# Gated mix of full and sliding attention: the prologue in five chunks, with other read-outs

## The chip, the cores and the metric

The kernel runs on one core of a Trainium2 chip. A core has five engines that run side by side: TensorE (PE in the profile) multiplies matrices into PSUM, VectorE (DVE) and ScalarE (ACT) compute element by element and read PSUM, GpSimd (POOL) does the same without PSUM, and SyncE (SP) here only issues DMAs. The metric is the device time of one execution in microseconds (us), of which the median of several runs is given. A time below is from the start of the profiled span unless it is called a length.

## The reference

Two attention layers read the same input `x` (1 x 2048 x 640, bf16) and their outputs are mixed by a gate. The core of it:

```python
g = sigmoid((x * gate_w).sum(-1, keepdims=True))
# A: full attention, 32 heads of 20
q, k, v = split(x @ A_wqkv)
a = merge(softmax(q @ k.T * 20**-0.5) @ v) @ A_wo
# B: each position attends to 8 positions, 2 apart, behind it
q, k, v = split(x @ B_wqkv)
idx = pos[:, None] - 2 * arange(8)          # masked where negative
b = merge(softmax(q . k[idx] * 20**-0.5) . v[idx]) @ B_wo
return g * a + (1 - g) * b
```

## The kernel before

The kernel writes every instruction as a task with the buffers that it reads and writes (`T`, L69). A small planner keeps a clock for each engine, and `emit` (L135) writes for each engine its tasks in the order in which they were made, with a semaphore wait for every task of another engine (and for a marked one of its own) on which one depends. So the order of tasks in the source is the order on each engine.

**The main part.** Heads go in eight groups of four ("quads"), queries in four blocks of 512, keys in 16 blocks of 128. One unit is one head, one query block and one key block: a score matmul of 32 rows into a PSUM bank (`mk_qk`, L994), the exponential of that bank on ScalarE (`mk_exp`, L1012), and a value matmul that adds to bank 5 (`mk_pv`, L1018). Units are taken three and two at a time in turn, from banks 0 to 2 and banks 3 and 4, 819 steps in all. Around them a greedy loop (L1175) places "lanes", which are generators with a due time: keys, queries and values of the later quads (`gen_k`, `gen_q`, `gen_v`), late constants and weights (`gen_late`, L594), and the whole of layer B. They share banks 6 and 7.

The softmax needs a bound instead of a row maximum: for every feature of a quad's keys the largest absolute value over all keys (`Kmax`, L409), and from it and the absolute query a bound that is subtracted from the scores. `mk_KM` (L414) takes the largest of the four chunk maxima and multiplies it by -1. `q_km` (L576) multiplies it with `qabs` and adds the result to the query's bank as one more feature, row 0 of each head, whose key is 1 (`e0`). So the first score needs the maximum over all keys of the first quad, and with it all of `x`.

**The prologue**, which the change is about, runs ahead of the planner's loop, in the order that its lines give:

- L320 to L333 issue the loads: from ACT's queue the first quad's key weights (80 columns), its query weights, and the gate vector `gw`; from SP's queue `x` in four chunks of 512 rows (L322), value weights of layer A (`WvA`, L331), the remaining key weights (L332) and query weights (L333). Layer B's weights follow (L595, L596).
- L335 to L360 make constants: the identity for transposes, zeros, ones in the value buffer (`vA`, L359, on VectorE). `pe_warm` (L343) runs ten matmuls on constants in bank 7.
- `pro_tr(t)` (L920) transposes chunk `t` of `x`, 20 blocks of 128 x 128, into three banks (0, 1, 2 or 3, 4, 7 in turn), and reads them out to `xT`: the first bank, two of the five feature blocks, by VectorE (L941), the other two by ScalarE (L938).
- `pro_k(t)` (L944) projects the keys of chunk `t` into bank 6 or 7 with five matmuls (L390), evacuates them to `kT` on ScalarE (L405) and takes their maxima from `kT` on VectorE (L410).
- L950 to L974 give the order: transposes 0 and 1, query weights (L372), keys 0, transposes 2, keys 1, the three Sel constants (`consts_late`, L362, used by layer B), transposes 3, the query matmuls of the first block into bank 0, keys 2, the query's read-out and absolute value (`q_abs`, L569), the gate vector's copy into column 1 of `WvA` (L962), keys 3, KM, six value chunks (`v_chunk`, L468, five matmuls each) in two banks with the KM matmuls between, and their read-outs (`v_evac`, L484, L495 and L503) on ScalarE. Then come the first two score groups (L1168, L1169) and the loop.

Column 1 of `WvA` makes the gate's logit come out of the same matmuls as the values of the first two quads (161 columns instead of 160).

Of the kernel before, what the change touches and what calls it, by code (L numbers as in the profile page):

```python
# [6 lines left out]
BF16 = mybir.dt.bfloat16  # L7
# [225 lines left out]
def _build(ctx, nc, A_x, A_wqkv, A_wo, B_wqkv, B_wo, gate_w, out):  # L233
# [33 lines left out]
    woBp = WvA  # L267
    gw = sb([P, CN], BF16, "gw")
    ident = sb([P, P], BF16, "ident")
# [42 lines left out]
    wB_v = B_wqkv.rearrange("(c p) f -> p c f", p=P)  # L312
    gw_v = gate_w.rearrange("(c p) -> p c", p=P)
    out_v = out[0].rearrange("(b p) d -> p b d", p=P)
# [5 lines left out]
    T("act", lambda e: e.dma_start(WqkA[:, :, D:D + 80], wA_v[:, :, D:D + 80]), writes=[("WkA", 0)], dma=True)  # L320
    for t in range(QCN):
        T("sp", lambda e, t=t: e.dma_start(x_tm[:, 4 * t:4 * t + 4, :], x_v[:, 4 * t:4 * t + 4, :]),  # L322
          writes=[("x_tm", t)], dma=True)
    T("act", lambda e: e.dma_start(WqkA[:, :, 0:80], wA_v[:, :, 0:80]), writes=[("WqA", 0)], dma=True)

    def sp_gw(e):
        with nc.allow_non_contiguous_dma(reason="tiny gate vector"):
            return e.dma_start(gw[:, :], gw_v)

    T("act", sp_gw, writes=["gw"], dma=True)  # L330
    T("sp", lambda e: e.dma_start(WvA[:, :, 2:D + 2], wA_v[:, :, 2 * D:3 * D]), writes=["WvA"], dma=True)  # L331
    T("sp", lambda e: e.dma_start(WqkA[:, :, D + 80:2 * D], wA_v[:, :, D + 80:2 * D]), writes=[("WkA", 1)], dma=True)  # L332
    T("sp", lambda e: e.dma_start(WqkA[:, :, 80:D], wA_v[:, :, 80:D]), writes=[("WqA", 1)], dma=True)  # L333

    T("pool", lambda e: e.iota(itmp, [[1, P]], base=0, channel_multiplier=-1), writes=["itmp"])  # L335
    T("pool", lambda e: e.iota(stmp, [[P, CN], [-DH, 32]], base=0, channel_multiplier=1), writes=["stmp"])
    T("dve", lambda e: e.memset(warm[:, :], 0.0), writes=["warm"])
    T("act", lambda e: e.activation(warm[:, 2:4], warm[:, 0:2], ACTF.Exp), reads=["warm"], writes=["warm2"])
# [4 lines left out]
    def pe_warm(e):  # L343
        ins = None
        for _ in range(10):
            ins = e.matmul(bank[7], ident[:, :], rgn[0][:, :, :].rearrange("p a b -> p (a b)"), start=True, stop=True)
        return ins

    T("pe", pe_warm, reads=["ident", "rgn"], writes=[("bk", 7)])
    T("dve", lambda e: e.memset(zt[:, :], 0.0), writes=["zt"])  # L350
# [3 lines left out]
    for i in range(2):  # L354
# [3 lines left out]
    T("dve", lambda e: e.memset(bank[OB], 0.0), writes=[("bk", OB)])  # L358
    T("dve", lambda e: e.memset(fap(vA, vA[:, 0, 0, 0:1], [[VW, NQUAD * KBN * 4], [1, 1]]), 1.0),  # L359
      writes=[("vA", q, g) for q in range(NQUAD) for g in range(6)])  # L360

    def consts_late():  # L362
        T("dve", lambda e: e.tensor_scalar(stmpf, stmp, 0.0, None, op0=ALU.is_ge), reads=["stmp"], writes=["stmpf"])
        T("dve", lambda e: e.tensor_scalar(Sel[:, :, :], stmp, float(DH), None, op0=ALU.is_ge),
          reads=["stmp"], writes=["Sel"])
        T("dve", lambda e: e.tensor_tensor(Sel[:, :, :], stmpf, Sel[:, :, :], ALU.subtract), reads=["stmpf"], writes=["Sel"])


# [44 lines left out]

    def mk_KM(q):  # L414
        T("dve", lambda e: e.tensor_reduce(Kmax[:, q % 2, 4:5], Kmax[:, q % 2, 0:4], AX.X, ALU.max),
          reads=[("Kmax", q % 2, t) for t in range(4)], writes=[("Kmax", q % 2, 4)], cost=160)
        T("dve", lambda e: e.tensor_scalar(KM[:, q:q + 1], Kmax[:, q % 2, 4:5], -1.0, None, op0=ALU.mult),
          reads=[("Kmax", q % 2, 4)], writes=[("KM", q)], cost=70)

# [48 lines left out]
    def v_chunk(b, p, gi, kb, i_):  # L468
        lo, hi = VG[gi]
        w0, wn = (1, 161) if p == 0 else (2 + 160 * p, 160)  # L470

        def fn(e):
            ins = None
            for c in range(CN):
                ins = e.matmul(bank[b][:, i_ * wn:(i_ + 1) * wn], xT[:, c, kb * P:(kb + 1) * P],  # L475
                               WvA[:, c, w0:w0 + wn], start=(c == 0), stop=(c == CN - 1))
            return ins

        rd = ["xT", "WvA"]
        if i_ == 0:  # L480
            return T("pe", fn, reads=rd, writes=[("bk", b)], cost=375)
        return T("pe", fn, reads=rd, accum=[("bk", b)], cost=375)
# [53 lines left out]
    def gen_k(q):  # L536
        yield ("dve", 370.0, 0.0)
        yield after(mk_wk(q))
        for tcc in range(4):
# [6 lines left out]
            kcount[q] = tcc + 1  # L546
        yield ("dve", 260.0, 0.0)
        mk_KM(q)
# [20 lines left out]
    def q_abs(b, gi):  # L569
        qt = qT[gi % NQT]  # L570
        T("dve", lambda e: e.tensor_copy(qt[:, :], bank[b]), reads=[("bk", b)], writes=[("qT", gi % NQT)], cost=690)  # L571
        return T("dve", lambda e: e.tensor_scalar(qabs[:, :].bitcast(I16), qt[:, :].bitcast(I16), 0x7FFF, None,
                                                  op0=ALU.bitwise_and),
                 reads=[("qT", gi % NQT)], writes=["qabs"], cost=300)
# [19 lines left out]
    def gen_late():  # L594
        T("sp", lambda e: e.dma_start(WqkB[:, :, :], wB_v[:, :, 0:2 * D]), writes=["WqkB"], dma=True)  # L595
        T("sp", lambda e: e.dma_start(WvBraw, wB_v[:, :, 2 * D:3 * D]),  # L596
          writes=["qB", "kB", "WvBraw"] + [("x_tm", t) for t in range(4)], dma=True)
        yield ("s", 4)
        for c in range(CN):
# [4 lines left out]
              cost=1290)  # L604
        latedone[0] = True
        for q in range(NQUAD):
            yield ("dve", 330.0, 0.0)
# [11 lines left out]
        for dp in range(CN):  # L619
            src = bass.AP(tensor=B_wo.tensor, offset=B_wo.offset + dp * D, ap=[[CN * D, 4], [DH * D, 32], [1, D]])  # L620
            T("sp", lambda e, dp=dp, src=src: e.dma_start(woBp[:, dp, 2:D + 2], src), writes=[("woBp", dp), "WvA"], dma=True)
            yield ("s", 2)
# [110 lines left out]
    def gen_F(tc):  # L733

        while not latedone[0] or (tc > 0 and not fdone.get(tc - 1)):
            yield ("poll",)
        xk = [("x_tm", t) for t in range(4)] if tc == 0 else []
        if tc == 0:
# [61 lines left out]
    def gen_K(tc):  # L800
# [3 lines left out]
        if tc == 0:  # L804
            T("dve", lambda e: e.memset(vB4[:, :, 0:PADB], 0.0), writes=["vB4"] + [("x_tm", t) for t in range(4)], cost=100)
        else:
# [113 lines left out]
    def pro_tr(t):  # L920
        bs = (0, 1, 2) if t % 2 == 0 else (3, 4, 7)
        for k, cs in enumerate(((0, 1), (2, 3), (4,))):
            b = bs[k]

            def pe_tr(e, t=t, cs=cs, b=b):
                ins = None
                for ci, c in enumerate(cs):
                    for i in range(4):
                        ins = e.transpose(bank_bf[b][:, ci * 512 + i * P:ci * 512 + (i + 1) * P],  # L929
                                          x_tm[:, 4 * t + i, c * P:(c + 1) * P], ident[:, :])  # L930
                return ins

            T("pe", pe_tr, reads=[("x_tm", t), "ident"], writes=[("bk", b)])
            n = len(cs)
            o_ap = xT[:, cs[0]:cs[0] + n, t * 512:(t + 1) * 512]
            i_ap = bank_bf[b][:, 0:n * 512].rearrange("p (a f) -> p a f", a=n)
            if k != 0:
                T("act", lambda e, o_ap=o_ap, i_ap=i_ap: e.activation(o_ap, i_ap, ACTF.Copy),  # L938
                  reads=[("bk", b)], writes=[("xTt", t, k)])
            else:  # L940
                T("dve", lambda e, o_ap=o_ap, i_ap=i_ap: e.tensor_copy(o_ap, i_ap),  # L941
                  reads=[("bk", b)], writes=[("xTt", t, k)])

    def pro_k(t):  # L944
        b = 6 + t % 2
        mm_part(b, proj_mms(b, WkP[0], t), 0, CN, [("WkP", 0)] + [("xTt", t, k) for k in range(3)], 1100)
        k_evac(b, 0, t, "act")
        k_red(0, t)

    pro_tr(0)  # L950
    pro_tr(1)
    mk_wq(0, 0)
    pro_k(0)
    pro_tr(2)
    pro_k(1)
    consts_late()
    pro_tr(3)
    QB0 = 0
    mm_part(QB0, proj_mms(QB0, WqP[0], 0), 0, CN, [("WqP", 0)] + [("xTt", 0, k) for k in range(3)], 1100)
    pro_k(2)  # L960
    q_abs(QB0, 0)
    T("dve", lambda e: e.tensor_copy(WvA[:, :, 1:2], gw[:, :].rearrange("p (c k) -> p c k", k=1)), reads=["gw", "WvA"],  # L962
      writes=["WvA"], cost=80)
    pro_k(3)
    sch.bufs["xT"] = sch.bufs[("xTt", 3, 2)]
    mk_KM(0)
    for i_ in range(3):
        v_chunk(3, 0, 0, i_, i_)
    q_km(QB0, 0)
    q_cp(QB0, 0)  # L970
    for i_ in range(3):
        v_chunk(4, 0, 1, 3 + i_, i_)
    for gi_ in range(2):
        v_evac(3 + gi_, 0, gi_, "act")  # L974
    for j in range(4):
# [18 lines left out]
    def mk_qk(s, again=0):  # L994
# [12 lines left out]
        for (qc, q, kb, j) in us:  # L1007
            rd.add(("kT", q, kb // 4))
            rd.add(("qT", (qc * NQUAD + q) % NQT))
        T("pe", fn, reads=sorted(rd, key=str), writes=[("bk", b0 + i) for i in range(len(us))], cost=315 + MM * again)  # L1010

# [156 lines left out]
    mk_qk(0)  # L1168
    mk_qk(1)  # L1169
    pend = []  # L1170
    pair_side = 0.0
# [176 lines left out]
```

## Time and profile before

| | us |
|---|---|
| median of three runs | 967.47 (967.17 to 969.41) |
| the profiled execution, its own time | 967.4 |
| its span, first to last instruction | 965.3 |
| busy in the span: TensorE / VectorE / ScalarE | 861.2 / 570.1 / 943.0 |
| first exponential of the main part starts | 22.1 |
| last value matmuls of the main part | 954.8 |
| TensorE idle before value matmuls L475, the first time | 1.4 |

The profile lists groups of equal instructions with busy time, mean length and the idle time of the engine ahead of them. The chain of waits is followed back from the last instruction: at each step to whatever released it. Between 22.1 and 952 us ScalarE is busy 929.0 of 929.9 us. Before 22.1 it is busy 11.1 us, TensorE 18.1 and VectorE 11.8. The DMA engines are busy without a break from about 3 to 24 us, at 280 to 400 GB/s: `x` is 2.6 MB, and the weights queue up behind it.

### The profile page before, as it was taken

The page shows a single profiled execution, that of the slowest core. Times are in us where ns is not written, and L with a number is a line of the kernel's source. Part 1 is how long each engine was busy: PE and PEld are TensorE (multiplying, and loading weights), DVE is VectorE, ACT ScalarE, POOL GpSimd, SP SyncE. Part 2 cuts the span into 40 slices and gives each one's busy share as a digit, 9 for nine tenths or more (in the row PEclk, how much of TensorE's full clock was granted, in tenths as well). Part 3 has the DMA queues.
Part 4 walks back from the last instruction along what each step waited for, and adds up shares of the span by engine and source line. Part 5 has one row for each costly group of instructions (what it writes and reads, how often), then busy time and mean ns, then how long its engine had stood idle before and what let it go on. Part 6 is the DMA issues. An engine that isn't in the chain of part 4 may idle for free.

```text
span 965.3 us, 16312 instructions
## 1 busy us (share of the span) xinstructions
PE 861.2 (89%) x6294; PEld 287.4 (30%) x6397; DVE 570.1 (59%) x1050; ACT 943.0 (98%) x842; POOL 0.7 (0%) x6
## 2 busy tenths in 40 slices
PE   7999999898898888889988889989989998999986
PEld 4333333322222222223322222332222233222332
DVE  4485443445524788762457798355789636987222
ACT  5999999999999999999999999999999999999995
POOL 0000000000000000000000000000000000000000
PEclk9999999999999999999999999999999999999999
DMA  9000000000000000000000000000000000000000
GB/s 312 3 2 21 15 1 1 1 22 14 1 1 1 1 1 1 2 1 7 15 8 1 1 1 1 8 8 7 8 1 1 1 9 14 8 1 1 1 1 28
DMA packets 11359, 12.84 MB, mean 13 GB/s; under 512 B 2708, under 2 KB 10644, under 8 KB 11284
## 3 DMA queue, kind: packets, MB, share of 16 engines
q1 hardware_dynamic: 9028, 11.27, 3.6%
q8 instruction: 52, 0.85, 0.4%
q10 hardware_dynamic: 2256, 0.53, 0.3%
q14 instruction: 23, 0.19, 0.1%
HBM read 9.18 MB, written 2.62 MB: 12 GB/s over the span
## 4 chain that ended last, share of the span: by engine, by line
ACT 73%; issue 17%; PE 8%; DVE 1%; DMA 1%; SPq 0%; DVEq 0%; ACTq 0%
ACT ebuf L1015 72%; PE ps L1002 3%; PE ps L1139 2%; PE ps L390 2%; PE ps L1023 1%; DMA x_tm<-in_A_x_dram 1%; DVE WvB L715 0%; ACT L_sb L838 0%; PE ps L929 0%; PE ps L475 0%; PE ps L765 0%; DVE rg L629 0%; DVE oTn L646 0%; DVE xT L941 0%; ACT kT L405 0%
## 5 line engine op out<-in xcount | busy, mean ns | idle before, releaser
L1015 ACT ACTIVATE ebuf<-ps 128x1536 bf16<-128x1536 f32 (+1 forms) x819 | 929.0, 1374 | 0.8
L1002 PE MATMUL ps<-qT,kT 32*128 32x512 bf16 x2068 | 322.1, 382 | 67.2 <-ACT ebuf L1015 53.6
L1002 PEld LDWEIGHTS ps<-qT,kT 32*128 32x128 bf16 x2068 | 88.9, 91 | 347.3 <-issue 141.6
L1023 PE MATMUL ps<-ebuf,vA 128*21 128x512 bf16 x2048 | 172.0, 382 | 0.6 <-ACT ebuf L1015 0.6
L1139 PE MATMUL ps<-xT,ident 128*128 128x512 bf16 x322 | 125.0, 389 | 16.3 <-PE ps L1002 6.3
L895 DVE TENSOR_TENSOR bw<-vB,bw 128x640 f32<-128x640 bf16 x112 | 91.8, 820 | 2.1
L899 DVE TENSOR_TENSOR blkacc<-blkacc,bw 128x640 f32<-128x640 f32 x96 | 79.0, 823 | 2.9
L629 DVE STREAM_TRANSPOSE rg<-ps 128x512 f32<-128x512 f32 x32 | 22.9, 717 | 93.4 <-PE ps L1023 93.4
L781 DVE TENSOR_TENSOR prod<-qk 128x512 bf16<-128x512 bf16 x160 | 57.3, 418 | 20.0 <-PE ps L765 19.8
L1139 PEld LDWEIGHTS ps<-xT,ident 128*128 128x128 bf16 x366 | 35.1, 96 | 98.9 <-PE ps L1139 59.3
L1023 PEld LDWEIGHTS ps<-ebuf,vA 128*21 128x21 bf16 x2048 | 42.0, 90 | 72.8 <-issue 50.3
L390 PE MATMUL ps<-xT,WqkB 128*128 128x512 bf16 x179 | 58.2, 384 | 2.2 <-PE ps L1002 1.4
L750 DVE CAST qk<-ps 128x512 bf16<-128x512 f32 x40 | 27.5, 687 | 48.1 <-PE ps L390 46.1
L390 PE MATMUL ps<-woA_r,oTn 128*128 128x320 bf16 x240 | 50.6, 302 | 0.1
L390 PE MATMUL ps<-xT,WqP 128*128 128x512 bf16 x148 | 43.1, 382 | 1.6 <-issue 0.6
L571 DVE CAST qT<-ps 128x512 bf16<-128x512 f32 x32 | 22.0, 688 | 37.7 <-PE ps L390 37.7
L390 PE MATMUL ps<-xT,WkP 128*128 128x512 bf16 x147 | 42.6, 382 | 1.9 <-issue 1.3
L402 DVE TENSOR_SCALAR kT<-ps,e 128x512 bf16<-128x512 f32 x28 | 21.0, 749 | 39.4 <-PE ps L390 39.3
L588 DVE CAST qT<-ps 128x512 bf16<-128x512 f32 x32 | 22.0, 688 | 23.2 <-PE ps L581 23.2
L390 PE MATMUL ps<-WvA,oBacc 128*128 128x320 bf16 x160 | 33.1, 301 | 0.5 <-PE ps L1002 0.4
L475 PE MATMUL ps<-WvA,xT 128*128 128x160 bf16 (+1 forms) x320 | 29.3, 233 | 1.4 <-DVE WvA L962 1.4
L813 DVE CAST vB<-ps 128x512 bf16<-128x512 f32 x20 | 13.7, 687 | 26.8 <-PE ps L390 26.5
(92 smaller groups left out, 471.9 us busy)
## 6 DMA issues: line engine op xcount, KB each, us to landing
x_tm<-in_A_x_dram SPq DMA_DIRECT2D x4, 640.0 KB
out_dram<-outsb SPq DMA_DIRECT2D x12, 160.0 KB
WqkB<-in_B_wqkv_dram SPq DMA_DIRECT2D x1, 1600.0 KB
WqkA<-in_A_wqkv_dram SPq DMA_DIRECT2D x2, 700.0 KB
WvA<-in_A_wqkv_dram SPq DMA_DIRECT2D x1, 800.0 KB
qk<-in_B_wqkv_dram SPq DMA_DIRECT2D x1, 800.0 KB
woA_r<-in_A_wo_dram SPq DMA_DIRECT2D x32, 25.0 KB
WvA<-in_B_wo_dram SPq DMA_DIRECT2D x5, 160.0 KB
```

Source lines behind the costliest of these rows:

```text
L390: ins = e.matmul(o, l, r, start=(k0 + k == 0), stop=(k0 + k == n - 1))
L475: ins = e.matmul(bank[b][:, i_ * wn:(i_ + 1) * wn], xT[:, c, kb * P:(kb + 1) * P], WvA[:, c, w0:w0 + wn], start=(c == 0), stop=(c == CN - 1))
L571: T("dve", lambda e: e.tensor_copy(qt[:, :], bank[b]), reads=[("bk", b)], writes=[("qT", gi % NQT)], cost=690)
L629: return T("dve", lambda e: e.transpose(rg[i][:, :], bank[OB]), reads=[("ob", j) for j in range(4)], writes=["rg"], cost=720)
L750: give(b, T("dve", lambda e, dst=dst, b=b: e.tensor_copy(dst, bank[b]), reads=[("bk", b)], writes=[key], cost=690))
L781: t = T("dve", lambda e, r=r, f=f, off=off: e.tensor_tensor(prod[r][:, :], qB[:, f, :], kB[:, f, off:off + 512], ALU.mult), reads=["qB", " ...
L895: T("dve", lambda e, vv=vv, av=av: e.tensor_tensor(tmpB, vv, av, ALU.mult), reads=[("aT", ai), "vB4"], writes=["tmpB"], cost=822)
L899: T("dve", lambda e: e.tensor_tensor(blkacc[:, :, :], blkacc[:, :, :], tmpB, ALU.add), reads=["tmpB"], writes=["blkacc"], cost=822)
L1002: ins = e.matmul(bank[b0 + i], kT[32 * j:32 * j + 32, q, kb * P:(kb + 1) * P], qT[gi % NQT][32 * j:32 * j + 32, :], start=True, stop=True)
L1015: return T("act", lambda e: e.activation(ebuf[s % NEB][:, 0:512 * n], ps[:, b0 * 512:(b0 + n) * 512], ACTF.Exp, scale=SCALE), reads=[("bk" ...
L1023: ins = e.matmul(bank[OB][32 * j:32 * j + DH + 1, :], vA[:, q, kb, VW * j:VW * j + DH + 1], ebuf[s % NEB][:, i * 512:(i + 1) * 512], start ...
L1139: T("pe", lambda e: e.matmul(bank[b], ident[:, :], xT[:, 0, 0:512], start=True, stop=True), reads=["xT", "ident"], writes=[("bk", b)], cos ...
```

## The change

All of it is in the prologue and in a few tasks that move out of it.

- `x` comes in five chunks of 256, 512, 512, 512 and 256 rows, and transposes, keys and maxima follow these chunks. A chunk of 512 uses banks 2, 3, 4 or 0, 1, 4 in turn, read out by VectorE, ScalarE and VectorE; a chunk of 256 uses banks 0 and 1, with three feature blocks read out by VectorE and two by ScalarE.
- Ten warm-up matmuls in bank 7 become seven in bank 0.
- Keys of all chunks but the last two are evacuated and reduced as before (bank 7). Those of the last two (banks 4 and 3) are reduced straight from PSUM; their evacuations by ScalarE follow the reductions.
- The first query block is projected later, behind keys 2, in two halves of 256 into banks 5 and 6, and is read out from both by one instruction. Its KM matmuls go by halves; one half is read out by VectorE and one by ScalarE.
- KM is one reduction without the factor -1; instead `qabs` gets its sign bit set where it was cleared.
- The gate vector is loaded straight into column 1 of `WvA`, without a copy. The load of `WvA` is split: 160 columns for the first two quads ahead, the others behind.
- Of the six value chunks three stay ahead of the first scores (bank 7, the third one behind the KM matmuls), and three go behind the first two score groups (bank 6, read out by VectorE).
- The ones in `vA` are written by POOL; the Sel constants are made in `gen_late`, behind the value weights of layer B.

```diff
-    for t in range(QCN):
-        T("sp", lambda e, t=t: e.dma_start(x_tm[:, 4 * t:4 * t + 4, :], x_v[:, 4 * t:4 * t + 4, :]),
+    CH = ((0, 256), (256, 512), (768, 512), (1280, 512), (1792, 256))
+    NCH = len(CH)
+    for t, (o_, n_) in enumerate(CH):
+        T("sp", lambda e, a=o_ // P, z=(o_ + n_) // P: e.dma_start(x_tm[:, a:z, :], x_v[:, a:z, :]),
           writes=[("x_tm", t)], dma=True)
...
-    T("act", sp_gw, writes=["gw"], dma=True)
-    T("sp", lambda e: e.dma_start(WvA[:, :, 2:D + 2], wA_v[:, :, 2 * D:3 * D]), writes=["WvA"], dma=True)
+    T("act", sp_gw, writes=["WvA1"], dma=True)
+    T("sp", lambda e: e.dma_start(WvA[:, :, 2:162], wA_v[:, :, 2 * D:2 * D + 160]), writes=["WvA0"], dma=True)
+    T("sp", lambda e: e.dma_start(WvA[:, :, 162:D + 2], wA_v[:, :, 2 * D + 160:3 * D]), writes=["WvA"], dma=True)
...
+    T("pool", lambda e: e.memset(fap(vA, vA[:, 0, 0, 0:1], [[VW, NQUAD * KBN * 4], [1, 1]]), 1.0),
+      writes=[("vA", q, g) for q in range(NQUAD) for g in range(6)])
...
-        for _ in range(10):
-            ins = e.matmul(bank[7], ident[:, :], rgn[0][:, :, :].rearrange("p a b -> p (a b)"), start=True, stop=True)
+        for _ in range(7):
+            ins = e.matmul(bank[0], ident[:, :], rgn[0][:, :, :].rearrange("p a b -> p (a b)"), start=True, stop=True)
...
+    def mk_KM(q, n=4):
+        T("dve", lambda e: e.tensor_reduce(KM[:, q:q + 1], Kmax[:, q % 2, 0:n], AX.X, ALU.max),
+          reads=[("Kmax", q % 2, t) for t in range(n)], writes=[("KM", q)], cost=160)
...
+        if n == 512:
+            parts = zip(((0, 1), (2, 3), (4,)), (2, 3, 4) if t % 2 else (0, 1, 4), ("dve", "act", "dve"))
+        else:
+            parts = zip(((0, 1, 2), (3, 4)), (0, 1), ("dve", "act"))
...
+    KB = (7, 7, 7, 4, 3)
...
+    def pro_kev(t):
+        a, n = CH[t]
+        b = KB[t]
+        return T("act", lambda e: e.activation(kT[:, 0, a:a + n], bank[b][:, 0:n], ACTF.Identity, bias=e0[:, 0:1]),
+                 reads=["e0"], accum=[("bk", b)], writes=[("kTt", t)])
...
+    def pro_k(t):
+        a, n = CH[t]
+        pro_kmm(t)
+        pro_kev(t)
+        pro_red(t, kT[:, 0, a:a + n], reads=[("kTt", t)])
+    def pro_k2(t):
+        pro_kmm(t)
+        pro_red(t, bank[KB[t]][:, 0:CH[t][1]], reads=[("bk", KB[t])])
+    QH = (OB, 6)
+    def pro_q():
+        for h in range(2):
+            b = QH[h]
+            mms = [(bank[b][:, 0:256], WqP[0][:, c, :], xT[:, c, 256 * h:256 * h + 256]) for c in range(CN)]
+            mm_part(b, mms, 0, CN, [("WqP", 0)] + xkeys[0] + xkeys[1], 600)
...
     pro_tr(0)
     pro_tr(1)
+    pro_k(0)
     mk_wq(0, 0)
-    pro_k(0)
     pro_tr(2)
     pro_k(1)
-    consts_late()
     pro_tr(3)
...
+    pro_tr(4)
     pro_k(2)
...
+    pro_q()
+    pro_k2(3)
+    pro_k2(4)
+    mk_KM(0, NCH)
+    pro_kev(3)
+    pro_kev(4)
+    for i_ in range(2):
+        v_chunk(7, 0, 0, i_, i_)
+    for h in range(2):
...
+        T("pe", fn, reads=["qabs", ("KM", 0)], accum=[("bk", b)], cost=MM)
...
+    v_chunk(7, 0, 0, 2, 2)
+    v_evac(7, 0, 0, "act")
...
     mk_qk(0)
     mk_qk(1)
+    for i_ in range(3):
+        v_chunk(6, 0, 1, 3 + i_, i_)
+    free_at[6] = v_evac(6, 0, 1).fin + 56.0
```

## The prediction

> **What bounds the kernel now.** I read the page first: its busy shares, the chain that ended last by engine, and the costliest group.
>
> ```profile
> span 965.3 us, 16312 instructions
> PE 861.2 (89%) x6294; PEld 287.4 (30%) x6397; DVE 570.1 (59%) x1050; ACT 943.0 (98%) x842; POOL 0.7 (0%) x6
> ACT 73%; issue 17%; PE 8%; DVE 1%; DMA 1%; SPq 0%; DVEq 0%; ACTq 0%
> L1015 ACT ACTIVATE ebuf<-ps 128x1536 bf16<-128x1536 f32 (+1 forms) x819 | 929.0, 1374 | 0.8
> ```
>
> ScalarE's 819 exponentials cost 929.0 us, and ScalarE stood idle 0.8 us before all of them together. Once they run, nothing can be won but that 0.8. So a change to the prologue is worth what it moves the first exponential, unless it makes the later order stall. The chain of waits, cut to the first 26 us, shows what sets that first one:
>
> ```profile
> 1.24 6.82 DMA x_tm<-in_A_x_dram
> ...
> 14.24 2.12 PE ps L390 x9
> 16.36 0.02 issue
> 16.38 0.70 ACT kT L405
> 17.08 0.02 issue
> 17.10 0.69 DVE Kmax L410
> 17.79 0.61 DVE qT L571
> ...
> 18.63 0.18 DVE WvA L962
> 18.81 0.05 issue
> 18.86 1.23 PE ps L475 x15
> 20.09 0.31 PE ps L581 x4
> 20.40 1.18 PE ps L475 x15
> 21.58 0.02 issue
> 21.60 0.57 ACT vA L495
> 22.18 0.06 ACT zg L503
> 22.24 4.52 ACT ebuf L1015 x4
> ```
>
> Columns: start, length, what. The reader is to see the end: a key evacuation, a maximum, the query read-outs, the gate copy, value matmuls, the max correction, more value matmuls, a value evacuation, then the first exponential at 22.24. Between the maximum's start (17.10) and that lie 5.14 us of short serial steps. The timeline of TensorE shows the front:
>
> ```profile
> 1.42 4.45 PE L346 MATMUL ps<-rgn,ident 128*128 128x512 bf16 x10 [1.42 <-DVE e L351]
> 5.69 1.66 PE L929 MATMUL ps<-ident,x_tm 128*128 128x128 bf16 x20
> 8.10 1.29 PE L929 MATMUL ps<-ident,x_tm 128*128 128x128 bf16 x20 [0.75 <-DMA x_tm<-in_A_x_dram]
> ```
>
> Ten warm-up matmuls start 427 ns apart. The first 20 transposes take 1.66 us, the next 1.29: counting starts in slices of 0.3 us, their pace doubles near 6.3 us, 4.9 us after TensorE began. The granted clock reads 1.00 in these slices all the same, so pace is the witness here.
>
> **The change, part by part.** I re-time the prologue by hand with the rows of before.
>
> *Five chunks of x.* Before, chunks land at 5.69 or just before, 8.05, 10.4 and 12.55 (waits of transposes for x): 0.64 MB each 2.35 us. At that pace rows to 256, 768, 1280, 1792 and 2048 land at about 4.5, 6.85, 9.25, 11.5 and 12.55. The last byte is no earlier; the last piece is half as large. One more x issue (0.45 to 0.88 us on SP) and one more for the split value weights push only the weights behind x on SP's queue: by the bytes moved, the key weights of the second quad are in at about 16 to 18, and their first reader stands at 21.06 before, some 19.5 now.
>
> *Seven warm-up matmuls.* They end 3 x 0.427 = 1.28 us earlier, at about 4.4; the first x then lands at 4.5. Ten cold transposes (0.107 each) run 4.5 to 5.6, then TensorE idles until 6.85. If the pace has doubled by then, transposes of chunk 1 end at 8.15, keys 0 at 8.75, transposes of chunk 2 run 9.25 to 10.55, keys 1 (5 x 0.216 = 1.08) to 11.6, chunk 3 to 12.9, chunk 4 (half of 1.29) to 13.55, keys 2 to 14.63. Keys 2 end at 16.36 before, since the query matmuls stood ahead of them; that is 1.7 us won.
>
> *Read-outs.* VectorE's 1024-wide one costs 0.69, ScalarE's 1.02 and 0.59 for 512. VectorE's 512 and 768 are not in the trace; they lie between the 0.17 of a five-element copy and 0.69, and I take 0.4 and 0.55, near the 0.39 of the 400-element copy and the 0.69 row. VectorE is then free at 14.75, ScalarE at 14.3. Key evacuation 2 runs 14.65 to 15.35, its maximum 15.4 to 16.1.
>
> *Query in two banks.* Ten half-width matmuls cost 1.08 if width decides (10 x 0.108) and 2.16 if each costs as much as a whole one; weight loads take 0.098 each in the row of L390, so I take 1.08: 14.63 to 15.75, hidden behind the maximum. Were it 2.16, query would end at 16.8 and keys 3 and 4 at 18.5, 0.7 late. The read-out from two banks (0.68) runs 16.1 to 16.8, the sign operation (0.29) to 17.1.
>
> *Maxima from PSUM.* Keys 3 end at 16.8 and keys 4 (half) at 17.35, both hidden behind VectorE. Reading 512 from PSUM in a maximum is not in the trace: between 0.68 (cast from PSUM) and 0.75 (L402), I take 0.69, and 0.42 for the last 256 (between 0.16 for four and 0.68 for 512): 17.1 to 17.8 to 18.2. The joined KM operation saves one of two 0.16 steps: KM at 18.36, against 19.76. The new wait: evacuations 3 and 4 on ScalarE now come after the maxima, 17.85 to 18.55 and (0.4) 18.95; behind them in ScalarE's queue stand the second query read-out, the value evacuation and the first exponential.
>
> *Gate column by DMA.* L962's copy (0.17) goes; value matmuls no longer wait for it but for two DMAs, and the KM matmuls stand behind them in TensorE's queue. The gate DMA lands 10.5 us after its issue at 1.88, at 12.4, and nothing needs it before 17.35. The new piece of value weights is 200 KB, behind x: at 375 GB/s it lands at 13.1; as slow as the 100 KB query weights of 160-byte rows (8.5 us) it lands at 21.0. I take 14, near the first bound, since it follows x on the same queue. A landing after 18.4 delays the end one for one, so the far bound costs 2.6 us.
>
> *The end.* Two value chunks (0.82) are done by 18.2, KM matmuls (0.31) run 18.45 to 18.8, the query halves are read out by VectorE to 19.2 and by ScalarE (0.4) 18.95 to 19.35; the third value chunk ends at 19.2. Score matmuls run 19.4 to 19.8. ScalarE's value evacuation (0.57 and 0.06) ends at 19.98, and the first exponential starts at 20.05. Three value chunks and an evacuation that stood on the path now follow the second score group; their 1.23 us fit where TensorE waited before (0.5 and 0.95 us idle ahead of the second and third score groups), with evacuation on VectorE, idle 4.33 us there. Without this cover the third exponential waits up to 0.7.
>
> *Off the path:* the ones of the value buffer go to POOL, busy 0.7 us in all; from 0.3 to 4 us (between a POOL iota of 160 elements at 0.27 and eight times VectorE's 0.485), needed at 19.4. Three Sel constants (0.8 us) go into the main part, where VectorE is 59% busy. One KM step fewer per quad saves nothing, as VectorE doesn't bound.
>
> Sum: 22.24 - 20.05 = 2.2 us. My hand-offs are near zero and rows say 0.02 to 0.25, so I allow 0.3 for a dozen: 1.9. The profiled run is 967.4 (span 965.3 and 2.1 around it), the median 967.47: 967.4 - 1.9 = 965.5.
>
> The pages bear on two places. "TensorE: Matmul & The Clock Gate", section "The HAM clock gate", of the Trainium skill says that half rate ends after a busy window of about 3.4 us whose phase is not tied to the kernel's start. It speaks against fewer warm-up matmuls: a window holding the new idle time might not count, and the estimate would be some 966.4 instead of 965.5. The trace agrees on halving (427 ns against 216), and shows 4.9 us to the rise.
>
> "DMA: Bandwidth & Descriptors", section "Specifications", wants pieces of 512 bytes or more for line rate; the 320-byte rows of the new weight piece break that. No run here shows what they cost.
>
> **The rivals.**
>
> *The clock rises later.* For: between 5.6 and 6.85 TensorE would idle before it has been busy 4.9 us. Against: a pause of 0.75 us before 8.10 left the pace fast. From 6.85 each microsecond at half pace makes TensorE half a microsecond late, less 0.5 that the wait for chunk 2 absorbs. If counting starts afresh at 6.85, the rise is at 11.75: (11.75 - 6.85)/2 - 0.5 = 1.95 lost, 967.4. A rise at 9.7, between the two, loses (9.7 - 6.85)/2 - 0.5 = 0.9: 966.4. Chance 0.27 for 966.0 to 967.4.
>
> *Slower: TensorE stays at half pace through the prologue.* Same place, but past 11.9 us, where loss equals gain, it is slower than before. The price at worst is the 10 us of matmuls from 6.85 to the last keys, taken twice, less 0.5 and less 0.45 that keys 4 wait for VectorE anyway: 9 us lost, 7 net, 974.5. Against: continuous work from 6.85 is longer than the 4.9 us that sufficed before. Chance 0.11 for 967.5 to 974.5.
>
> *More than I see.* If chunks land sooner (x moves at 300 GB/s before, 390 later) and ScalarE's tail is shorter, the first exponential comes at 19.2: 964.4, or with the 0.8 us idle gone 963.6. For: half the last chunk. Against: VectorE's queue from 15.4 on depends little on landing. Chance 0.18 for 963.0 to 964.8.
>
> *The value weights land late* (21.0): 965.5 + 2.6 = 968.1. Chance 0.03.
>
> **How the numbers follow.** The forecast case, 964.8 to 966.0, has 0.41. The range reaches down into the third rival and up past the whole first and the late weights: 964.0 to 968.4. A measurement of this kernel can tell about 0.3%, or 2.9 us, from no change: faster than 964.5 gets 0.16 (most of the third rival), slower than 970.4 gets 0.08 (the worse half of the second), the rest 0.76.
>
> **What would show it.** The first exponential near 20 us in the chain; KM near 18.4; transposes of chunk 1 in 1.3 and not 2.1 us; keys 2 ending near 14.6; the two maxima on PSUM at 0.69 and 0.42, back to back after the sign operation; no wait of value matmuls for a DMA; idle time before the exponentials still about 0.8 us. The main part's order is generated anew; if that idle time grows by more than 1 us, or the pace doubles after 9 us, the prediction is wrong.

## The result, and the profile after

| | before | after |
|---|---|---|
| median of 12 runs each, us | 968.45 (967.17 to 970.05) | 965.64 (964.40 to 967.39) |
| ratio, 95% interval | | 0.9972 (0.9964 to 0.9980) |
| profiled execution, its time / span | 967.4 / 965.3 | 965.52 / 963.7 |
| first exponential of the main part | 22.12 | 19.51 |
| from it to the last quad's L629 | 933.1 | 934.1 |

The change takes 0.28% (0.20 to 0.36), or 2.8 us. The forecast was 965.5, from 967.4. Two executions below stand outside all medians and spans, one of the kernel before (1253.58 us) and one of the variant with one warm-up matmul (1752.59 us). The page of the changed kernel, the lines that answer to those of before:

```profile
span 963.7 us, 16441 instructions
PE 881.2 (91%) x6408; PEld 287.5 (30%) x6408; DVE 570.4 (59%) x1047; ACT 941.6 (98%) x839; POOL 3.1 (0%) x7
L1076 ACT ACTIVATE ebuf<-ps 128x1536 bf16<-128x1536 f32 (+1 forms) x819 | 929.5, 1370 | 1.3
```

The main part's exponentials cost what they did (929.0 before); the idle time ahead of them rose from 0.8 to 1.3. Now the chain of waits, from the third x chunk to the first exponential (start, length, what):

```profile
1.74 7.58 DMA x_tm<-in_A_x_dram
9.33 0.05 issue
9.37 1.29 PE ps L934 x20
10.66 1.08 PE ps L386 x5
11.74 1.68 PE ps L934 x30
13.42 1.09 PE ps L386 x5
14.51 0.02 issue
14.53 0.70 ACT kT L961
15.23 0.02 issue
15.25 0.69 DVE Kmax L965
15.94 0.61 DVE qT L990
16.55 0.02 issue
16.57 0.29 DVE qabs L992
16.86 0.94 DVE Kmax L965 x2
17.81 0.02 issue
17.83 0.17 DVE KM L411
18.00 0.04 issue
18.05 0.38 PE ps L1020 x8
18.43 0.47 PE ps L469 x5
...
18.99 0.57 ACT vA L489
19.56 0.06 ACT zg L497
19.62 6.46 ACT ebuf L1076 x6
```

The reader is to see that keys 2 (L386, 13.42) now end at 14.51 and not at 16.36, that both last maxima (L965 x2) come straight behind the sign operation (L992), that no gate copy is left, and that one value chunk (L469 x5) stands in this chain where two groups of three (L475 x15) stood before.

The profile has one thing more. The main part is 1.0 us longer than before. I compared the starts of L629, the transposition that ends each of the 32 groups: after minus before is -2.47 to -2.49 us for the first nine, -1.31 for the tenth, -1.57 for the eleventh and between -1.44 and -1.79 from there on. The loss is one event, and busy times by stage show it (columns: stretch, its length, busy time and instructions of PE, PEld, DVE, ACT and POOL, granted clock, DMA share, GB/s):

```profile
300.00:306.00 6.00, 5.69 (x41) 1.80 (x38) 3.80 (x3) 6.00 (x6) 0.00 (x0) 1.00 0.01 3
306.00:308.00 2.00, 0.98 (x6) 0.24 (x5) 0.71 (x1) 2.00 (x4) 0.00 (x0) 1.00 0.00 0
308.00:309.00 1.00, 0.68 (x10) 0.37 (x12) 1.00 (x1) 1.00 (x2) 0.00 (x0) 0.93 0.00 0
309.00:312.00 3.00, 3.00 (x21) 0.45 (x14) 0.77 (x2) 2.86 (x3) 0.00 (x0) 0.50 0.00 0
312.00:313.00 1.00, 1.00 (x9) 0.20 (x8) 0.30 (x1) 0.95 (x2) 0.00 (x0) 0.87 0.00 0
```

At 306.00 ScalarE computes layer B's exponential (L838) between two of the main part's; TensorE, which waits for the next one, is busy 0.98 of 2 us. Then its granted clock falls to 0.50: with 0.93 in 308 to 309 and 0.87 in 312 to 313 it is low for 0.14 + 3 + 0.26 = 3.4 us, and ScalarE is no longer busy throughout. The profile of before has the same hole behind its L838 at 308.5, and no fall.

### The profile page after: what moved, and what is told of

It reads as the page before. It is cut to its first block, busy times and chain, and to the rows that moved or that the text cites. A ratio compares the mean times of both kernels' runs of the same rounds, so it can differ in the third digit from the quotient of the medians.

```text
span 963.7 us, 16441 instructions
## 1 busy us (share of the span) xinstructions
PE 881.2 (91%) x6408; PEld 287.5 (30%) x6408; DVE 570.4 (59%) x1047; ACT 941.6 (98%) x839; POOL 3.1 (0%) x7
## 4 chain that ended last, share of the span: by engine, by line
ACT 73%; issue 17%; PE 8%; DVE 1%; DMA 1%; SPq 0%; DVEq 0%; ACTq 0%
ACT ebuf L1076 72%; PE ps L1061 2%; PE ps L1200 2%; PE ps L386 1%; PE ps L1084 1%; DMA x_tm<-in_A_x_dram 1%; DVE WvB L715 0%; ACT L_sb L838 0%; PE ps L934 0%; DVE Kmax L965 0%; DVE rg L629 0%; DVE oTn L646 0%; PE ps L765 0%; DVE rgn L643 0%; PE ps L865 0%
## 5 line engine op out<-in xcount | busy, mean ns | idle before, releaser
L1200 PE MATMUL ps<-xT,ident 128*128 128x512 bf16 x366 | 142.0, 389 | 9.7
L629 DVE STREAM_TRANSPOSE rg<-ps 128x512 f32<-128x512 f32 x32 | 22.9, 717 | 94.8 <-PE ps L1084 94.8
L386 PE MATMUL ps<-xT,WqkB 128*128 128x512 bf16 x200 | 64.1, 387 | 0.0
L386 PE MATMUL ps<-woA_r,oTn 128*128 128x320 bf16 x240 | 50.6, 302 | 0.0
L386 PE MATMUL ps<-xT,WqP 128*128 128x512 bf16 (+1 forms) x165 | 45.6, 376 | 0.7 <-DVE WqP L368 0.5
L386 PE MATMUL ps<-xT,WkP 128*128 128x512 bf16 (+1 forms) x165 | 45.5, 376 | 0.0
L582 DVE CAST qT<-ps 128x512 bf16<-128x512 f32 x31 | 21.4, 689 | 22.2 <-PE ps L575 22.1
L386 PE MATMUL ps<-WvA,oBacc 128*128 128x320 bf16 x160 | 33.1, 301 | 0.4 <-PE ps L1061 0.4
L386 PE MATMUL ps<-xT,WvB 128*128 128x512 bf16 x100 | 31.7, 380 | 0.0
```

The source lines that it names most:

```text
L386: ins = e.matmul(o, l, r, start=(k0 + k == 0), stop=(k0 + k == n - 1))
L582: return T("dve", lambda e: e.tensor_copy(qT[gi % NQT][:, :], bank[b]), reads=[("bk", b)], writes=[("qT", gi % NQT)], cost=690)
L629: return T("dve", lambda e: e.transpose(rg[i][:, :], bank[OB]), reads=[("ob", j) for j in range(4)], writes=["rg"], cost=720)
L1200: T("pe", lambda e: e.matmul(bank[b], ident[:, :], xT[:, 0, 0:512], start=True, stop=True), reads=["xT", "ident"], writes=[("bk", b)], cos ...
```

## The experiments

Times are medians, with the ratio to runs of the kernel before on the same chip. "First" is the start of the first exponential in the profile, "KM" the start of that instruction; 19.51 and 17.83 in the changed kernel, 22.12 and (its first step) 19.41 before. One profile of a variant is one draw, and the next run shows how far two draws differ. Fences of edits are shortened to the lines that matter.

**The changed kernel again.**

> The changed kernel once more, for a second profile. Theory: the prologue's gain repeats (first exponential of the main part at 19.3 to 19.8 us, 22.1 before), and the 1.2 us that the main part lost between 307 and 313 us, where the granted TensorE clock read 0.50, is chance: this time it is absent or at another place, and the main part from the first to the last exponential lasts 932.4 to 933.8 us. Rival: the main part's newly generated order loses it, so the loss of 1.2 us stands at the same place again.

965.56 us, ratio 0.9967 (0.9954 to 0.9980). Half of it missed: the fall at 308 is absent and the main part lasts 933.3 us to the last L629, but the first exponential came at 20.26, KM at 18.58. TensorE's timeline (start, length):

```profile
4.74 1.22 PE L934 MATMUL ps<-ident,x_tm 128*128 128x128 bf16 x10
6.93 2.31 PE L934 MATMUL ps<-ident,x_tm 128*128 128x128 bf16 x20 [0.96 <-DMA x_tm<-in_A_x_dram]
10.10 1.31 PE L934 MATMUL ps<-ident,x_tm 128*128 128x128 bf16 x20
```

and in the first profile of the same kernel:

```profile
4.74 0.86 PE L934 MATMUL ps<-ident,x_tm 128*128 128x128 bf16 x10
7.05 1.29 PE L934 MATMUL ps<-ident,x_tm 128*128 128x128 bf16 x20 [1.45 <-DMA x_tm<-in_A_x_dram]
```

Twenty transposes in 2.31 us are half pace: here the pace doubled only at about 10.2 us, in the other profile at about 5.1. That is the rival "the clock rises later", in one and the same kernel, and it costs 20.26 - 19.51 = 0.75 us. So TensorE's clock comes in twice: in the prologue of the changed kernel, and in holes of the main part.

**Fillers in layer B's holes.**

```diff
-  ... ACTF.Exp, scale=SCALE), reads=["L"], writes=["L"], cost=1060)
+  ... ACTF.Exp, scale=SCALE), reads=["L"], writes=["L"], cost=1060); [idle_mm() for _ in range(4)]
```

> The changed kernel with four added filler matmuls on TensorE at each of the four places where ScalarE computes layer B's softmax exponential (L838) between two of the main part's. Theory: the 0.9 us hole that L838 leaves on TensorE can let its clock fall to half for 3.4 us, which costs about 1.2 us when it happens; filled, the granted clock stays at 1.00 from 20 to 950 us in the profile, the times spread less than the 3 us of the changed kernel, and the median is 0.3 to 1.2 us lower than the changed kernel's. Rival: fillers delay the score matmuls behind them or change nothing in the clock: median equal or up to 1 us higher, spread as before.

965.87 us, 0.9966 (0.9953 to 0.9978). The profile has no fall from 20 to 950 us, and five times spread over 1.35 us, but the median is no lower: inconclusive on the time. Three of its five spans (964.0 to 964.3) still lie about 1 us above the other two (962.9 and 963.2); no trace shows what those three lost. The fillers' own price shows: the main part lasts 933.6 where kernels without a fall have 933.1 to 933.3 (0.36 of it at the sixteenth group, behind the second place).

**A further version.** Edit, on top of the fillers:

```diff
-    pro_k(2)
+    pro_k2(2)
+    pro_kev(2)
     pro_q()
...
-    for i_ in range(2):
-        v_chunk(7, 0, 0, i_, i_)
+    v_chunk(7, 0, 0, 0, 0)
...
-    v_chunk(7, 0, 0, 2, 2)
-    v_evac(7, 0, 0, "act")
...
     mk_qk(1)
+    for i_ in range(1, 3):
+        v_chunk(7, 0, 0, i_, i_)
+    free_at[7] = v_evac(7, 0, 0).fin + 56.0
```

> The filled kernel, with chunk 2's maximum also taken from PSUM (its evacuation behind it), one value chunk instead of three ahead of the first scores, and all value read-outs of the first two groups on VectorE. Theory: VectorE's queue bounds KM, and ScalarE's value read-out delays the first exponential; KM moves from 17.8 to about 17.45 and the first exponential from 19.5 to 19.0, so 0.5 us less than the filled kernel. Rival: TensorE's keys 3 and 4 bound KM, and the first scores end no sooner: 19.4 to 19.6.

965.96 us, 0.9966 (0.9954 to 0.9978): no better. The first exponential came at 19.39, KM at 17.76. The rival is right:

```profile
15.64 1.04 PE ps L386 x4
16.68 0.02 issue
16.70 0.70 DVE Kmax L965
...
18.07 0.47 ACT kT L961
18.54 0.28 ACT qT L1029
18.82 0.14 issue
18.96 0.59 PE ps L1059 x5
```

Maximum 3 starts when keys 3 (L386) end, so TensorE is the next bound, and ScalarE's evacuations behind the maxima hold the second query half. Five value chunks behind the second score group also bring the third exponential's scores into the chain, at a cost of 0.03 us.

**One warm-up matmul instead of seven.**

```diff
-        for _ in range(7):
+        for _ in range(1):
```

> The changed kernel with one warm-up matmul instead of seven. Theory of the clock: TensorE idles from about 1.9 to 4.7 us and again to 7.05, so its pace doubles only at 10 to 12 us; transposes of chunk 1 take 2.1 us instead of 1.3, and the first exponential comes 1.2 to 2 us later, at 20.8 to 21.6. Rival: the pace doubles at a time that does not depend on the warm-up: first exponential at 19.3 to 19.8, as with seven.

966.24 us over seven executions, 0.9975 (0.9965 to 0.9986). As the theory of the clock has it: first exponential at 21.46, two chunks at half pace:

```profile
6.98 2.32 PE L934 MATMUL ps<-ident,x_tm 128*128 128x128 bf16 x20 [1.30 <-DMA x_tm<-in_A_x_dram]
10.15 2.34 PE L934 MATMUL ps<-ident,x_tm 128*128 128x128 bf16 x20
13.53 1.84 PE L934 MATMUL ps<-ident,x_tm 128*128 128x128 bf16 x30
```

1.95 us later than with an early rise, 1.20 later than with the late one.

The eighth execution, of 1752.59 us (span 1750.7), has a mean granted clock that reads 1.000 where the seven others read 0.998, and no trace. TensorE is busy 859.6 us in the profile of this variant, nearly all of it at full pace; twice that, some 1720 us as an estimate, fits a TensorE that stayed at half pace to the end, with the clock reading 1.00 as it does here ahead of the rise. This would be the prediction's second rival, far beyond its worst price of 974.5. Whether the single warm-up matmul brought it about, one execution can't show.

**Parts of the change undone, one at a time.**

```diff
# order_back
-    pro_k(2)
-    pro_q()
+    pro_qmm()    # the query's matmuls
+    pro_k(2)
+    pro_qrd()    # its read-out and sign
# max_back
-    pro_k2(3); pro_k2(4); mk_KM(0, NCH); pro_kev(3); pro_kev(4)
+    pro_k(3); pro_k(4); mk_KM(0, NCH)
# values_back
+    for i_ in range(3):
+        v_chunk(4, 0, 1, 3 + i_, i_)
     v_evac(7, 0, 0, "act")
+    v_evac(4, 0, 1, "act")
...
     mk_qk(1)
-    for i_ in range(3):
-        v_chunk(6, 0, 1, 3 + i_, i_)
-    free_at[6] = v_evac(6, 0, 1).fin + 56.0
# four_chunks
-    CH = ((0, 256), (256, 512), (768, 512), (1280, 512), (1792, 256))
+    CH = ((0, 512), (512, 512), (1024, 512), (1536, 512))
...
-        for _ in range(7):
+        for _ in range(10):
...
```

> The changed kernel with the query's ten matmuls ahead of keys 2 again; VectorE's order stays. Theory: keys 2 then end 1.1 us later, and everything behind their maximum on VectorE with them: maximum 2 at 16.3, KM at 18.9, first exponential at 20.6 (1.1 later than 19.5). Rival: the maxima from PSUM are what pays, and VectorE catches up: first exponential at most 0.4 later.

> The changed kernel with the maxima of the last two key chunks taken from their evacuated copies again, as for the other chunks. Theory: keys 3 end at 16.5, their evacuation at 17.25, the two maxima at 18.4, so KM comes 0.5 later (18.4); ScalarE is free earlier, so the first exponential comes 0.4 to 0.5 later, at 20.0. Rival: with evacuations out of the way of ScalarE's second query half, nothing is lost: 19.4 to 19.6.

> The changed kernel with all six value chunks ahead of the first scores and both read-outs on ScalarE. Theory: the three added chunks (1.23) stand in TensorE's queue ahead of the first scores, and the second read-out ahead of the first exponential: 20.7, 1.2 later. Rival: they fit where TensorE waits for KM, at most 0.3 later.

> The changed kernel with x in four chunks of 512 rows and ten warm-up matmuls, as before; the last chunk's maximum is taken from PSUM. Theory: the last 512 rows land at 12.55 and their 20 transposes end 0.6 to 0.7 later than with a short last chunk, so keys 2, the maxima and the first exponential come 0.5 to 0.6 later, at 20.1. Rival: one reduction less on VectorE makes up for it: 19.5 or sooner.

| run | median, ratio (95%) | KM | first | later than 19.51 | expected |
|---|---|---|---|---|---|
| order_back | 966.87, 0.9981 (0.9970 to 0.9992) | 19.09 | 20.76 | 1.25 | 1.1 |
| max_back | 965.94, 0.9968 (0.9956 to 0.9979) | 18.50 | 20.17 | 0.66 | 0.4 to 0.5 |
| values_back | 967.93, 0.9991 (0.9980 to 1.0002) | 17.84 | 20.52 | 1.01 | 1.2 |
| four_chunks | 965.95, 0.9974 (0.9964 to 0.9984) | 18.20 | 19.87 | 0.36 | 0.5 to 0.6 |

All four profiles have the pace doubled before chunk 1, so the first exponentials compare. Each theory holds within 0.25 us and each rival falls, by the first exponential; the times alone (intervals of some 2 us) could not tell max_back or four_chunks from the changed kernel. (before_early_fill, below, has the prologue of before unchanged and its first exponential at 22.26 instead of 22.12: two draws of one prologue differ by 0.14 even where the clock rises early in both.) The four losses add to 3.28, more than the whole 2.61: the parts overlap. order_back's profile has a fall too, from 309.8 to 313.2 us, behind L838 as in the first profile of the changed kernel; after_again, one_warm, max_back and four_chunks have the same hole and no fall.

values_back lost more time than its 1.0 us. Its main part is 935.5 long, and its clock fell twice, first here (same columns):

```profile
22.50:23.00 0.50, 0.34 (x4) 0.25 (x4) 0.00 (x0) 0.50 (x2) 0.00 (x0) 0.87 1.08 376
23.00:26.00 3.00, 3.00 (x13) 0.86 (x12) 0.89 (x2) 2.64 (x3) 0.00 (x0) 0.50 0.51 173
```

just behind the hole which the value chunks fill in the changed kernel, and again at 650.9, behind L838.

**Parts of the change alone, in the kernel before.**

```diff
# before_order
+    pro_k(2)
     mm_part(QB0, proj_mms(QB0, WqP[0], 0), ...)
-    pro_k(2)
     q_abs(QB0, 0)
# before_max: pro_k2 reduces from the bank, makes KM, then evacuates
-    pro_k(3)
+    pro_k2(3)
...
-    mk_KM(0)
# before_order_max: both
```

> The kernel before with one edit: keys 2 projected ahead of the query. Theory (each part of the change is worth little alone, because another queue is late next): maximum 2 comes 1.0 earlier, but maximum 3 still waits for the evacuation of keys 3 and comes 0.5 earlier, and the value matmuls stand ahead of the scores: first exponential 0.6 to 0.7 earlier, at 21.5 (22.1 before). Rival: the 1.7 us that keys 2 are earlier in the changed kernel come from the order alone, and the end follows: 20.5 to 20.8.

> The kernel before with one edit: the last chunk's maximum taken from PSUM, its evacuation behind it. Theory: nothing is won, as VectorE reaches that maximum at 18.7 only, 0.5 after the evacuation's end: first exponential at 22.0 to 22.2. Rival: a step of 0.7 leaves the chain: 21.4 to 21.6.

> The kernel before with both of these edits. Theory: KM comes 0.9 earlier (18.5), but the value matmuls then stand in front: first exponential 0.8 to 1.0 earlier, at 21.2, more than the two edits' sum by 0.2 to 0.3. Rival: both together bring most of the change's 2.6: 20.0 or sooner.

| run | median, ratio (95%) | first | earlier than 22.12 | expected |
|---|---|---|---|---|
| before_order | 967.72, 0.9990 (0.9979 to 1.0000) | 21.61 | 0.51 | 0.6 to 0.7 |
| before_max | 968.37, 0.9993 (0.9984 to 1.0002) | 22.33 | -0.21 | 0 |
| before_order_max | 968.12, 0.9987 (0.9978 to 0.9997) | 21.14 | 0.98 | 0.8 to 1.0 |

The maximum from PSUM alone wins nothing (its -0.21 is hardly more than the 0.14 between two draws), the order alone 0.5, both 1.0: each step uncovers the queue behind it. before_order_max's profiled run then lost 2.3 us between the first exponential and the first L629 (its clock read 0.50 from 24.1 to 30.9 us), so its 0.98 was gone again in that run.

**Fillers in the early hole of the kernel before.** The hole is TensorE's two waits ahead of the second and the third score group, in the profile of before:

```profile
22.38 0.39 PE L1002 MATMUL ps<-qT,kT 32*128 32x512 bf16 x2 [0.49 <-ACT zg L503]
23.72 0.40 PE L1002 MATMUL ps<-qT,kT 32*128 32x512 bf16 x3 [0.95 <-ACT ebuf L1015]
```

```diff
-    mk_qk(1)
+    mk_qk(1); T("pe", ...)    # four matmuls of ident and xT into bank 7
```

> The kernel before with one edit: four filler matmuls between the second and the third score group, where TensorE idles 0.49 and 0.95 us and where the changed kernel puts three value chunks. Spans of the kernel before fall on three levels, about 965.4, 966.4 and 967.8 us, with mean clocks of 0.998, 0.9965 and 0.9945. Theory: one of the two falls of the clock that a 967.8 span holds starts in this hole (as at 22.9 and 24.2 us in two profiles of kernels with all values ahead of the scores), and the value chunks that moved there also took this fall away. Then no span is above 967.0, and the median of times is 0.5 to 1.3 us lower than that of the kernel before. Rival: the falls come from layer B's exponentials alone; spans near 967.8 remain in a third of the runs, and the median is within 0.4.

967.61 us, 0.9990 (0.9980 to 0.9999), 0.6 below the median of before measured beside it (968.24). Eleven of twelve spans are 965.4 to 965.8, one is 967.1; of 16 spans of before on that chip seven are 965.4 to 965.6, five 966.3 to 966.6 and four 967.6 to 967.9. In these runs filling the early hole thus took away most of the time lost on the upper levels. My statement that none is above 967.0 failed by one run, and that both levels go, not only the upper one, is more than I expected: why a filled early hole also spares the later falls stays open.

## Why the prediction was right

**The number.** That 965.64 lies so near 965.5 is in part luck. In the first profile the prologue won 2.61 and not 1.9, the main part lost 1.0 that the prediction put at nothing, and the time around the span was 1.8 instead of 2.1. In the second the pace doubled after 9 us, which the prediction had named as a sign of being wrong; the time was 965.78 all the same, since that main part had no fall.

**The bound.** Right: a change to the prologue is worth the first exponential's move, 2.61 us in the first profile and 1.86 in the second. Wrong was "nothing can be won but that 0.8" in the main part. Idle time ahead of exponentials in one profile without a fall does not show what a fall takes in another run: 0.9 to 1.1 us, or 2.3 in the long one. Over all experiments, spans of the kernel before lie on three levels near 965.5, 966.5 and 967.8, about a third of 82 runs on each, with mean clocks of 0.998, 0.9966 and 0.9943. One fall of 3.4 us lowers the mean over 966 us by 0.0018 and two by 0.0035 (an estimate), which fits one and two falls; the kernel before itself has a trace of the lowest level alone. The changed kernel's 17 spans are 962.6 to 962.9 (three) and 963.6 to 963.9 (fourteen). From lowest level to lowest level (965.5 to 962.8) that is 2.7 us, from mean to mean (966.6 and 963.6) 3.0. The 967.47 that the prediction stood on, and its profile, came from the lowest level of before; twelve runs gave 968.45. So 1 us of the 2.8 is the kernel before being slower than its three runs said.

**The sum.** It gave 20.05 and allowed 0.3 on top; the first profile has 19.62 in the chain's terms. Chunks landed 0.04 to 0.2 later than worked out (7.05, 9.37, 11.54 against 6.85, 9.25, 11.5), without harm. Keys 2 ended at 14.51 (14.63). The steps mis-sized: maximum 2 to the sign operation's end took 1.61 us and not 1.7, the two maxima from PSUM 0.94 and not 1.11, since VectorE's instructions overlap by up to 0.09 each; KM came at 17.83 instead of 18.2 to 18.36. The allowance for hand-offs wasn't needed; they are 0.02 to 0.05 in the chain. The terms that were bounded from both sides: read-outs of 768 0.56 (0.55 taken), of 256 0.42 by VectorE and 0.38 by ScalarE (0.4), the ten half-width query matmuls 1.1 (1.08, not 2.16), the POOL memset 2.47 (0.3 to 4).

**The moved value chunks.** Right on the path: undone, the first exponential is 1.0 later. But the step priced the hole they moved into only as cover. It also lets the clock fall, by the profiles of values_back and before_order_max, and fillers there alone take 0.6 us off the median of before. So the change probably gains there a second time, which the prediction didn't see; no run measures the two gains apart.

**The weights by DMA.** Right: value matmuls started at 17.05, straight behind the keys, and the profile has no wait of theirs for a DMA. So the 320-byte rows cost nothing that the path shows. The Trainium skill's "DMA: Bandwidth & Descriptors", section "Specifications", asks for 512 bytes or more for line rate; what rate this piece had, no run here measures.

**The clock in the prologue.** The forecast took the early rise, and the rival priced a rise near 9.7 us at 0.9. Both happen in the same kernel: early with 19.51, at about 10.2 us with 20.26, 0.75 later. The rival's formula would have given (10.2 - 6.85)/2 - 0.5 = 1.2 for this rise, so its price was too high. All six profiles with ten warm-up matmuls (before, its four variants and four_chunks) have the rise between 4.5 and 7.1 us; of the seven with seven, six have it between 5.1 and 6.0 and one at 10.2 (by the clock records of the traces, with which the pace agrees where matmuls run). Whether ten would have prevented the late one wasn't run alone, and one warm-up matmul makes it worse by another 1.2. The rise of before came 5.1 us after TensorE's first matmul, those of the changed kernel's two profiles 3.7 and 8.8 us after it: "TensorE: Matmul & The Clock Gate", section "The HAM clock gate", of the Trainium skill says that the phase of its window is not tied to the kernel's start, and these agree with it. That section's table has the clock fall after an idle window of about 3.4 us; here it fell with TensorE idle no longer than 1 us at a time, and busy for 1.8 to 2.3 of the 3.4 us before each fall, so here the measurement decides. The length of the window shows in the falls: 3.4 us in five of them, twice that in the sixth. What decides whether such a stretch brings a fall stays open: over the 3.41 us ahead of the fall at 308.9 TensorE was busy 2.08 us, and in max_back, around the same hole (306.4 to 309.8), 2.07 without a fall.

## What to carry to other kernels

When one engine's queue bounds a prologue, re-time every queue by hand: an edit that shortens one step is worth nothing until the queue behind it is short too (0.5, 0 and 1.0 us for two edits alone and together). Read the same landmark, group by group, in two profiles: a constant offset with one jump tells a prologue's gain from an event in the main part. And look at TensorE's holes even where another engine bounds: a hole of 1 us is free, until the clock falls behind it.

## What the runs showed of the hardware

- TensorE's granted clock fell to 0.50 without a long idle time: behind 0.98 busy us of 2 at 306 us, behind waits of 0.49 and 0.95 at 20.3 to 22.1 (values_back), and at 651.5 in before_max. A half-busy stretch isn't enough by itself: before was busy 1.98 of the 3.41 us from 16.74 and kept its clock. It stayed low 3.4 us in five falls, once 6.8, and cost 0.9 to 1.1 us, once 2.3, in a kernel that ScalarE bounds.
- Whether it falls differs from run to run of the same kernel, and spans of one kernel lie on levels 1.0 to 1.3 us apart. A median of three runs can sit on one of them.
- The granted clock in the rows reads 1.00 from 6 to 10 us of after_again, where the pace of transposes (2.31 against 1.29 us for 20) shows half speed.
- The clock changes on a grid: from the rise to the first fall it was 17.07 us in values_back and 303.79 in the first profile of the changed kernel, 5 and 89 times the 3.413 us that a fall lasted.
- A maximum over 512 fp32 values read from PSUM by VectorE takes what one over 512 bf16 values in SBUF takes: 0.69 us (four_chunks, both forms).
